# Moving one small tile so that the tiles behind it start at multiples of 128 bytes

## The chip, the cores and the metric

The kernel runs on one core of a Trainium2 chip. The metric is the time of one execution on the device in microseconds (us). The kernel before takes 977.99 us, the median of three runs (977.63 to 978.67). In the profile PE is TensorE's matmuls, PEld its weight loads (LDWEIGHTS), DVE VectorE, ACT ScalarE, POOL GpSimd, SP SyncE, whose queue issues most DMAs.

## The reference

An attention over 32 inducing vectors, a second one back to the tokens, and two MLPs without bias, each with a hidden width of 2048, for 12480 tokens of width 128:

```python
def mab(q, kv):
    s = scale * (q @ kv.transpose(0, 2, 1))
    s = s - s.max(-1, keepdims=True)
    a = np.exp(s)
    a /= a.sum(-1, keepdims=True) + 1e-09
    return a @ kv
h = mab(I, x)                    # I: 32 x 128
x = mab(x, h)                    # 12480 x 128
h = x @ w_in;   x = (h * np.cos(h)) @ w_out                      # MLP 1
h = x @ w_in2;  x = (h * (1.0 / (1.0 + np.exp(-h)))) @ w_out2    # MLP 2
```

The weights come in as float64 and are narrowed on the core.

## The kernel before

The tokens are cut into 98 tiles of 128 (the last has 64). A prologue (up to about 49 us) loads x, transposes it into the tiles xF, held (as x1) and xT, runs the first attention, and multiplies its result h, kept as hT4, with the first MLP's input weights. The four tiles hw0 to hw3 hold that product, so the second attention's output needn't be formed: the main loop multiplies hw with stk, the second attention's weights for a block of tokens.

The main loop works on 26 blocks of tokens. 22 of them are 512 columns wide; of the last four, two are 320 and two are 288 wide. Each block has 8 units, a unit being 256 of the 2048 hidden channels, in two halves. One step of the loop holds, in this order on TensorE:

- `mlp1_in` (line 739): 2 matmuls of unit s, stationary hw, moving stk
- `mlp2_in` (line 878): 6 matmuls of unit s - 11, stationary wi2, moving yhi and ylo
- `mlp2_out` (line 825, in `down`): 6 matmuls of unit s - 13, stationary wo2, moving hi2 and lo2
- `mlp1_out` (line 825, in `down`): 6 matmuls of an earlier unit (s - 1), stationary wo1, moving hi1 and lo1

Between them ACT and DVE form h cos h and its split into hi and lo (lines 782, 788, 794, 815), and ACT and POOL form the Silu and its split (893, 901, 902). A product is of two float32r numbers, each split into a high and a low part, and takes three matmuls for each half: first weights with hi, second weights with hi, first weights with lo. So wo1 is two tiles, wo1_0 and wo1_1, and so are wo2 and wi2. The first 12 units of MLP 1 and the first 8 of MLP 2 use plain float32 weights instead (wf1, and held as wf2; line 835). Six times in the loop the softmax of a further chunk of tokens is worked in ("take" multiplies hT4 with columns of held or xT); around these steps the order of the groups differs, since `mlp2_in` is then held back behind `mlp2_out` or behind `mlp1_out`.

The order is written out by hand (`manual_schedule`). The tiles that live through the whole program come from one pool, `persist`, which lays them out in the order in which they are asked for and rounds each up to a multiple of 32 bytes in a partition. `flag` is one number that the end of the prologue writes (a bound on the size of the cosine's argument); all engines read it once, at line 1037, to choose between the two forms of the main loop.

Of the kernel before, what the change touches and what calls it, by code (L numbers as in the profile page):

```python
# [11 lines left out]
I32 = mybir.dt.int32  # L12
# [9 lines left out]
def tile_induced_attention_then_two_mlps(  # L22
# [58 lines left out]
    persist = ctx.enter_context(tc.tile_pool(name="persist", bufs=1))  # L81

    half_pi = persist.tile([P, 1], F32, name="half_pi")
    quarter = persist.tile([P, 1], F32, name="quarter")
    s_w = persist.tile([P, 1], F32, name="s_w")
    hT4 = persist.tile([C, G, M], F32, name="hT4")

    held = persist.tile([P, G * W], F32, name="held")
# [3 lines left out]
    wf1 = persist.tile([P, NF, C], F32, name="wf1")  # L92
    hw = [persist.tile([P, FF // 4], F32R, name=f"hw{i}") for i in range(4)]
    wo1 = [persist.tile([P, NF, C], F32R, name=f"wo1_{i}") for i in range(2)]
    flag = persist.tile([1, 1], I32, name="flag")
    stk = persist.tile([P, 2, W], F32R, name="stk")

    sft = {
# [980 lines left out]
```

## Time and profile before

| | |
|---|---|
| median of three runs | 977.99 us (977.63 to 978.67) |
| span of the profiled execution | 977.7 us |
| PE (matmuls) busy | 960.4 us, 98% |
| PEld (weight loads) busy | 772.6 us, 79% |
| DVE busy | 787.5 us, 81% |
| ACT busy | 702.6 us, 72% |
| POOL busy | 508.7 us, 52% |
| chain that ended last | PE 95%, DVE 3%, ACT 1%, POOL 1% |
| granted TensorE clock, mean | 0.998 |

A matmul's record lasts longer than its share of the engine, since the next one starts before it ends. So the busy time says that PE is never without work, and the start times of the timeline say at what rate it does it. The timeline merges neighbours of one group; it gives the start of the first and their count. Both `mlp2_out` and `mlp1_out` are line 825 there: in a step the first group of 4 + 2 is wo2, the second is wo1.

### The profile page before, as it was taken

What the parts mean: (1) busy time and instruction counts of PE and PEld (TensorE: products, weight loads), DVE (VectorE), ACT (ScalarE), POOL (GpSimd) and SP (SyncE); (2) the same over time, 40 slices, a digit from 0 to 9 for tenths busy, and PEclk for the clock granted to TensorE, in tenths of its full rate; (3) what the DMA queues carried; (4) which work ended last, traced back from release to release, by engine and by line L of the source; (5) the groups of instructions that cost most, each with busy time, mean ns of one, the idle gap of its engine ahead of it and who ended that gap; (6) DMA issues with size and microseconds to landing.
All of it is one profiled execution on the core that took longest, in us unless ns stands there. A gap on an engine that the chain in (4) does not pass through costs nothing.

```text
span 977.7 us, 12404 instructions
## 1 busy us (share of the span) xinstructions
PE 960.4 (98%) x4663; PEld 772.6 (79%) x4663; DVE 787.5 (81%) x818; ACT 702.6 (72%) x764; POOL 508.7 (52%) x265
## 2 busy tenths in 40 slices
PE   8898999999999999999999999999999999999997
PEld 6544677888887888887888887888887888889997
DVE  4888887988878888888888888888888888867881
ACT  5777677777667777767777776877766877777775
POOL 1234454664554655555655555555555555565555
PEclk9999999999999999999999999999999999999999
DMA  9331010010010010010100100100100100000000
GB/s 352 107 117 49 18 22 5 7 33 11 12 22 6 17 22 5 18 22 1 23 19 4 22 17 5 22 12 11 22 11 12 22 11 8 18 17 12 14 8 17
DMA packets 65230, 28.22 MB, mean 29 GB/s; under 512 B 54312, under 2 KB 59784, under 8 KB 65160
## 3 DMA queue, kind: packets, MB, share of 16 engines
q1 hardware_dynamic: 64504, 27.24, 10.7%
q8 instruction: 39, 0.64, 0.3%
q14 instruction: 31, 0.25, 0.1%
q10 hardware_dynamic: 656, 0.09, 0.1%
HBM read 14.79 MB, written 6.39 MB: 22 GB/s over the span
## 4 chain that ended last, share of the span: by engine, by line
PE 95%; DVE 3%; ACT 1%; POOL 1%; issue 0%; ACTq 0%; POOLq 0%
PE acc L825 52%; PE h L878 27%; PE h L739 9%; PE acc L835 3%; PE pt L371 1%; PE hp L519 1%; PE s L201 1%; PE s L404 1%; PE spin L327 0%; DVE sign L147 0%; ACT c L782 0%; POOL held L155 0%; ACT s L893 0%; DVE sign L144 0%; DVE hi L794 0%
## 5 line engine op out<-in xcount | busy, mean ns | idle before, releaser
L902 POOL TENSOR_TENSOR lo<-s,hi 128x1024 fp32r<-128x1024 f32 (+2 forms) x197 | 448.4, 2276 | 379.8 <-ACT hi L901 353.8
L825 PE MATMUL acc<-hi,wo 128*128 128x512 f32 (+2 forms) x1584 | 409.7, 380 | 0.0
L825 PEld LDWEIGHTS acc<-hi,wo 128*128 128x128 f32 x1584 | 288.2, 188 | 58.8 <-issue 3.4
L788 DVE TENSOR_TENSOR h<-h,c 128x1024 f32<-128x1024 f32 (+2 forms) x196 | 227.5, 1161 | 130.4 <-ACT c L782 130.0
L782 ACT ACTIVATE c<-h,half_pi 128x1024 f32<-128x1024 f32 (+2 forms) x208 | 221.5, 1065 | 150.2 <-PE h L739 150.2
L893 ACT ACTIVATE s<-h 128x1024 f32<-128x1024 f32 (+2 forms) x208 | 202.5, 973 | 73.6 <-PE h L878 68.3
L878 PE MATMUL h<-yhi,wi 128*128 128x512 f32 (+2 forms) x832 | 246.8, 378 | 3.9 <-ACT s L893 3.9
L825 PE MATMUL acc<-lo,wo 128*128 128x512 f32 (+2 forms) x792 | 235.4, 378 | 0.1
L794 DVE CAST hi<-h 128x1024 fp32r<-128x1024 f32 (+2 forms) x196 | 226.2, 1154 | 6.8
L815 DVE TENSOR_TENSOR lo<-h,hi 128x1024 fp32r<-128x1024 f32 (+2 forms) x196 | 225.1, 1149 | 5.7
L901 ACT CAST hi<-s 128x1024 fp32r<-128x1024 f32 (+2 forms) x197 | 196.8, 999 | 6.3
L878 PEld LDWEIGHTS h<-yhi,wi 128*128 128x128 f32 x832 | 152.2, 188 | 33.7 <-ACT s L893 4.8
L825 PEld LDWEIGHTS acc<-lo,wo 128*128 128x128 f32 x792 | 145.7, 188 | 29.9 <-POOL lo L907 0.4
L878 PE MATMUL h<-ylo,wi 128*128 128x512 f32 (+2 forms) x416 | 157.1, 378 | 0.0
L739 PE MATMUL h<-stk,hw 128*128 128x512 f32 (+2 forms) x416 | 127.0, 386 | 2.0 <-DVE c L788 1.3
L739 PEld LDWEIGHTS h<-stk,hw 128*128 128x128 f32 x416 | 76.0, 188 | 26.8 <-issue 7.1
L878 PEld LDWEIGHTS h<-ylo,wi 128*128 128x128 f32 x416 | 78.2, 188 | 14.5
L859 ACT CAST yhi<-acc 128x512 fp32r<-128x512 f32 (+2 forms) x26 | 14.6, 560 | 15.7 <-PE acc L825 13.9
L925 DVE STREAM_TRANSPOSE o<-acc 128x512 f32<-128x512 f32 (+2 forms) x26 | 17.5, 674 | 6.8 <-PE acc L825 6.8
L835 PE MATMUL acc<-c,wf 128*128 128x512 f32 x48 | 22.5, 591 | 0.0
L860 DVE TENSOR_TENSOR ylo<-acc,yhi 128x512 fp32r<-128x512 f32 (+2 forms) x26 | 16.9, 650 | 5.1 <-ACT yhi L859 5.1
L155 POOL TENSOR_TENSOR win<-sign,tail 128x512 int32<-128x512 int32 x4 | 5.1, 1281 | 27.3 <-DVE sign L147 20.8
(143 smaller groups left out, 344.3 us busy)
## 6 DMA issues: line engine op xcount, KB each, us to landing
out_dram<-o SPq DMA_DIRECT2D x80, 64.0 KB, 1.9
x_sb<-in_x_dram SPq DMA_DIRECT2D x8, 512.0 KB, 9.6
raw<-in_moe_w_in_dram SPq DMA_DIRECT2D x8, 512.0 KB, 5.6
raw<-in_moe_w_out_dram SPq DMA_DIRECT2D x8, 512.0 KB, 3.8
stk<-ahi SPq DMA_DIRECT2D x40, 64.0 KB, 2.0
stk<-at SPq DMA_DIRECT2D x40, 64.0 KB, 2.0
x_sb<-in_x_dram SPq DMA_DIRECT2D x3, 256.0 KB, 3.6
x_sb<-in_x_dram SPq DMA_DIRECT2D x2, 320.0 KB
```

The source lines that it names most:

```text
L739: nc.tensor.matmul(ps[:, a, 0:n], lhsT=hw[f // 4][:, f % 4 * P : (f % 4 + 1) * P], rhs=stacks[b][:, 0:n], start=True, stop=True,)
L782: nc.scalar.activation(cs, h, AF.Sin, bias=half_pi, scale=1.0)
L788: nc.vector.tensor_tensor(cs if whole else h, h, cs, ALU.mult)
L794: nc.vector.tensor_copy(hi[:, :, 0:n], h)
L815: nc.vector.tensor_tensor(lo[:, :, 0:n], h, hi[:, :, 0:n].bitcast(F32), ALU.subtract)
L825: nc.tensor.matmul(acc[:, 0:n], lhsT=wt[:, 2 * j + a, :], rhs=gt[:, a, 0:n], start=(j == 0 and p == 0 and a == 0), stop=(j == NJ - 1 and p ...
L835: nc.tensor.matmul(acc[:, 0:n], lhsT=w[:, 2 * j + a, :], rhs=c[:, a, 0:n], start=(j == 0 and a == 0), stop=(j == NJ - 1 and a == 1),)
L878: nc.tensor.matmul(ps[:, a, 0:n], lhsT=wt[:, fs], rhs=yt[:, 0:n], start=(p == 0), stop=(p == 2),)
L893: nc.scalar.activation(sv, hid2.pop(u)[:, :, 0:n], AF.Silu)
L901: nc.scalar.copy(hv, sv)
L902: nc.gpsimd.tensor_tensor(lv, sv, hv.bitcast(F32), ALU.subtract)
L925: nc.vector.transpose(o.rearrange("p t d -> p (t d)")[:, 0:n], acc2.pop(b)[:, 0:n])
```

## The change

The line that asks for `flag` moves from behind `wo1` to ahead of `hT4`:

```diff
     s_w = persist.tile([P, 1], F32, name="s_w")
+    flag = persist.tile([1, 1], I32, name="flag")
     hT4 = persist.tile([C, G, M], F32, name="hT4")
 ...
     wo1 = [persist.tile([P, NF, C], F32R, name=f"wo1_{i}") for i in range(2)]
-    flag = persist.tile([1, 1], I32, name="flag")
     stk = persist.tile([P, 2, W], F32R, name="stk")
```

The instructions, their order and their waits are the same in both built programs. The start addresses within a partition, in bytes, are:

| tile | before | past a multiple of 128 | after | past a multiple of 128 |
|---|---|---|---|---|
| half_pi, quarter, s_w | 16512, 16544, 16576 | 0, 32, 64 | the same | |
| flag | 95968 | 96 | 16608 | 96 |
| hT4 | 16608 | 96 | 16640 | 0 |
| held | 17120 | 96 | 17152 | 0 |
| xT | 25312 | 96 | 25344 | 0 |
| wf1 | 63200 | 96 | 63232 | 0 |
| hw0 to hw3 | 71392, and on by 2048 | 96 | 71424, and on by 2048 | 0 |
| wo1_0, wo1_1 | 79584, 87776 | 96 | 79616, 87808 | 0 |
| stk | 96000 | 0 | the same | |
| hi1, lo1, hi2, lo2, yhi, ylo | 132992 to 192384 | 0 | the same | |
| wi2_0, wi2_1 | 196480, 204672 | 0 | the same | |
| wo2_0, wo2_1 | 212864, 221056 | 0 | the same | |

One LDWEIGHTS of hw, wo1, wi2 or wo2 reads 128 columns, which are 512 bytes of a partition, at a multiple of 512 bytes from its tile's start.

## Rows read from the trace of the kernel before

**Rows 1.** The page: busy us by engine; granted clock in 40 slices; chain that ended last.

```profile
PE 960.4 (98%) x4663; PEld 772.6 (79%) x4663; DVE 787.5 (81%) x818; ACT 702.6 (72%) x764; POOL 508.7 (52%) x265
...
PEclk9999999999999999999999999999999999999999
...
PE 95%; DVE 3%; ACT 1%; POOL 1%; issue 0%; ACTq 0%; POOLq 0%
```

**Rows 2.** Busy time in 640 to 740 us: length, engines (instructions), clock, DMA, GB/s.

```profile
640.00:740.00 100.00, 100.00 (x437) 81.76 (x436) 83.31 (x72) 71.21 (x69) 53.90 (x23) 1.00 0.08 17
```

**Rows 3.** Timeline of PE, one wide step: start us, length us, line, tiles, count.

```profile
797.16 0.62 PE L739 MATMUL h<-stk,hw 128*128 128x512 f32 x2
797.62 0.63 PE L878 MATMUL h<-yhi,wi 128*128 128x512 f32 x2
...
798.31 0.62 PE L878 MATMUL h<-yhi,wi 128*128 128x512 f32 x2
...
798.99 1.07 PE L825 MATMUL acc<-hi,wo 128*128 128x512 f32 x4
...
800.35 1.10 PE L825 MATMUL acc<-hi,wo 128*128 128x512 f32 x4
...
801.75 0.62 PE L739 MATMUL h<-stk,hw 128*128 128x512 f32 x2
```

**Rows 4.** Timeline of PE, the start of hw's group in two steps eleven apart.

```profile
792.57 0.39 PE L739 MATMUL h<-stk,hw 128*128 128x512 f32 x1
...
843.09 0.39 PE L739 MATMUL h<-stk,hw 128*128 128x512 f32 x1
```

**Rows 5.** Groups by line and shape: count, busy us, mean ns, idle us before.

```profile
L825 PEld LDWEIGHTS acc<-hi,wo 128*128 128x128 f32 x1584 | 288.2, 188 | 58.8 <-issue 3.4 <-DVE h L788 1.0 <-DVE hi L794 0.5
...
L878 PEld LDWEIGHTS h<-yhi,wi 128*128 128x128 f32 x832 | 152.2, 188 | 33.7 <-ACT s L893 4.8 <-ACT wi L181 0.2 <-issue 0.2
...
L739 PEld LDWEIGHTS h<-stk,hw 128*128 128x128 f32 x416 | 76.0, 188 | 26.8 <-issue 7.1 <-DVE c L788 3.4 <-ACT stk L682 0.9
```

**Rows 6.** Timeline of PE, a step with narrow MLP 1 and wide MLP 2.

```profile
882.47 0.75 PE L825 MATMUL acc<-hi,wo 128*128 128x320 f32 x4
...
883.35 0.46 PE L739 MATMUL h<-stk,hw 128*128 128x320 f32 x2
883.64 0.61 PE L878 MATMUL h<-yhi,wi 128*128 128x512 f32 x2
...
885.00 1.07 PE L825 MATMUL acc<-hi,wo 128*128 128x512 f32 x4
```

**Rows 7.** Timeline of PE, a step at a softmax chunk, with wo2 behind hw.

```profile
171.92 0.63 PE L739 MATMUL h<-stk,hw 128*128 128x512 f32 x2
172.39 1.09 PE L825 MATMUL acc<-hi,wo 128*128 128x512 f32 x4
...
173.77 0.62 PE L878 MATMUL h<-yhi,wi 128*128 128x512 f32 x2
...
175.13 1.10 PE L825 MATMUL acc<-hi,wo 128*128 128x512 f32 x4
```

**Rows 8.** Timeline of PE behind a hold-up: wo2's group, wi2's, then wo1's.

```profile
149.26 1.09 PE L825 MATMUL acc<-hi,wo 128*128 128x512 f32 x4
...
150.65 0.62 PE L878 MATMUL h<-yhi,wi 128*128 128x512 f32 x2
...
152.03 0.86 PE L825 MATMUL acc<-hi,wo 128*128 128x512 f32 x3
```

**Rows 9.** Groups by line and shape, other engines on moved and unmoved tiles.

```profile
L155 POOL TENSOR_TENSOR tail<-sign,tail 128x512 int32<-128x512 int32 x4 | 5.1, 1287 | 6.4 <-DVE sign L147 6.4
...
L155 POOL TENSOR_TENSOR wf<-sign,tail 128x512 int32<-128x512 int32 x4 | 5.1, 1280 | 22.1 <-DVE sign L147 19.8 <-ACT tail L141 2.3
...
L181 ACT CAST wi<-tail 128x512 fp32r<-128x512 f32 x4 | 2.5, 616 | 0.6 <-POOL tail L155 0.6
L181 ACT CAST wo<-wf 128x512 fp32r<-128x512 f32 x4 | 2.5, 614 | 0.0
```

## The prediction

> **What bounds the kernel now.** I read the page first: its busy shares, the granted clock and the chain that ended last [rows 1]. TensorE's matmuls are busy for 960.4 of 977.7 us, the clock is at its upper level (2.4 GHz) in all 40 slices, and 95% of the chain is PE. The window view of a steady stretch [rows 2] says the same more sharply: in 100 us PE is busy for 100.00, DVE for 83.31, ACT for 71.21, POOL for 53.90, and the DMA engines have a share of 0.08. So in the main loop only the distance from one matmul's start to the next one's counts. I call it the spacing. A busy PE says nothing of it, since matmuls overlap (one is recorded with some 390 ns and the next starts 230 ns after it), so the third view is the timeline of PE alone, whose start times give the spacing.
>
> One step of the loop is 20 matmuls of 512 columns in four groups [rows 3]. From start to start they take: hw (L739, 2 matmuls) 797.16 to 797.62 = 0.46 us, wi2 (L878, 6) 797.62 to 798.99 = 1.37, wo2 (L825, the first 6) 798.99 to 800.35 = 1.36, wo1 (L825, the last 6) 800.35 to 801.75 = 1.40. Per matmul that is 230, 228, 227 and 233 ns. wo1 and wo2 run the same line with the same shapes and both read moving tiles at multiples of 128 bytes, and yet wo1 costs 0.04 us a step more. Within wi2 the first three matmuls take 0.69 us (797.62 to 798.31) and the last three 0.68. Over eleven steps [rows 4] a step is (843.09 - 792.57) / 11 = 4.593 us.
>
> **What the change does.** The built program has the same instructions in the same order with the same waits; only addresses change. Ten tiles, from hT4 to the second wo1, move 32 bytes up, from 96 past a multiple of 128 to a multiple; the flag takes the gap of 32 bytes that this leaves ahead of hT4. Of what the main loop touches in every step, two sets of tiles move: hw and wo1, both stationary operands of TensorE. Everything else in the loop (stk, the hi and lo tiles, yhi and ylo, wi2, wo2, raw) stays where it is, at multiples of 128. So the trace of before holds the comparison already: weights at 96 (hw, wo1) against weights at 0 (wi2, wo2), in one loop at one clock.
>
> *The load itself.* LDWEIGHTS is recorded with 188 ns for L739, L825 and L878 alike [rows 5]. No difference is to be seen there, and it lies beside the matmul before it. If the address costs anything it is in the spacing.
>
> *The spacing by weights.* wo2 at 0: 1.36 / 6 = 226.7 ns. wo1 at 96: 1.40 / 6 = 233.3. For wi2 at 0 the question is why it is not at 226.7 too. Where the blocks are 320 columns wide for hw and wo1 and still 512 for wi2 and wo2 [rows 6], wi2 takes 883.64 to 885.00 = 1.36, so 226.7 as well. And in a step whose order is changed by a softmax step [rows 7], where wo2 and not wi2 stands behind hw, it is wo2 that is slow (172.39 to 173.77 = 1.38) and wi2 that is at the floor (173.77 to 175.13 = 1.36). So the extra goes with hw and wo1 and with the few matmuls right behind them, whichever tile those read, and not with the place in the step or with what DVE, ACT and POOL do at that moment. I take 226.7 ns as the spacing that a train of weights at multiples of 128 settles at.
>
> *The sum.* At 226.7 a step is 20 x 0.2267 = 4.533 us; it is 4.593 now; the gain is 0.060 us. Steps in which hw, wi2, wo2 and wo1 all run with 512 columns: 22 wide blocks of 8 units less the 12 plain-fp32 units at the front, 164. 164 x 0.060 = 9.8 us. The front steps that run hw and wi2 only gain 0.46 + 1.37 - 8 x 0.2267 = 0.016 each, about 0.2 us for 12. The narrow blocks gain nothing: wo1 and hw together take 882.47 to 883.64 = 1.17 us for 8 matmuls of 320 columns, 146 ns, and 0.29 of it is hw at 145. Against it stands a transient: after each hold-up of PE at a softmax step a train starts slow (1.39 + 1.38 us for 12 matmuls [rows 8], 0.05 above the floor); I allow ten such trains (two for each of five softmax steps in the wide part), 0.5 us, which stay as they are. 9.8 + 0.2 - 0.5 = **9.5 us**.
>
> *The rest.* Other instructions that touch moved tiles run in the prologue and the first blocks. ACT's cast to wo1 from wf1 (both at 96) takes 614 ns, to wi2 from tail (both at 0) 616; POOL's join to wf1 1280, to tail 1287 [rows 9]. That is bounded by -7 and +2 ns an instruction over a few dozen, under 0.3 us either way; I take 0, nearest to ACT's pair. No DMA reads or writes a moved tile. The flag is read once per engine at the branch; its address is still a multiple of 4, and I take 0.
>
> *What is late next.* A step shorter by 1.3% puts DVE at 83.31 / 0.987 = 84.4% and ACT at 72% [rows 2]; neither becomes the bound, so the gain is not caught by a wait.
>
> The profiled span is 977.7 us, 0.3 below the median of 977.99, so a gain out of the trace can be taken off the median: 977.99 - 9.5 = **968.5 us**.
>
> **The rivals.**
>
> *B, the address is not what costs.* hw and wo1 differ from wi2 and wo2 in more than 96 bytes: they lie low in the partition (71 to 96 KB against 196 to 229 KB) and are read against other moving tiles (stk, hi1, lo1). If one of these makes the 233 ns, it stays, and the time is 977.99 + 0. For it: no tile of the trace lies low and at a multiple of 128, so rows can't part the two; and the load's 188 ns [rows 5] don't see the address. Against it: hw and wo1 are six tiles at six places between 71 and 88 KB, read against different moving tiles, and both sets are above 226.7. The Trainium skill (SBUF — State Buffer, Specifications (TRN2)) gives SBUF 16-byte lines and a penalty for each step to a new one. By that rule a row of 512 bytes that starts at 96 covers as many lines as one that starts at 0, nothing changes and the time is 978.0, which is this rival. The trace speaks against it only so far as wo1 and wo2, both on 16-byte boundaries, differ by 7 ns.
>
> *C, the slow train stays: slower.* There is a second spacing for weights at 0. Behind a hold-up wo2 and wi2 run at 1.39 + 1.38 us for 12 matmuls = 231 ns [rows 8], and in the steps of rows 3 the train is back at 226.7 within a few matmuls. If the return is owed to the mixture of groups in a step, and with all weights alike nothing pulls the train back, every matmul is at 231: 20 x 0.231 = 4.62 us a step, 0.027 more than 4.593, x 164 = +4.4 us, **982.4**. It decides the other way from a spacing above 4.593 / 20 = 229.7 ns. Against it: in all wide steps the train of wi2 and wo2 does come back to 226.7 within three to twelve matmuls, and nothing in the rows shows it leaving again without a hold-up.
>
> *D, half of it.* Only the loads' own extra goes (wo1 to 1.36, 0.04 a step) and the transient behind hw stays, because it comes from hw's short group or the change of moving tile: 164 x 0.04 = 6.6 less the 0.5 as above, some 6 us, 972.
>
> **How the numbers follow.** Forecast A (968.5; itself 966 to 971, since start times are rounded to 10 ns and an error of 0.015 us in the step's 4.533 is 2.5 us over 164 steps): 0.70. D 0.07, B 0.14, C 0.09. The range goes from the low end of A over D and B, 966.0 to 979.0, and leaves out C and a little of A's tails. What a measurement of this kernel can tell from no change is about 0.2%, 2 us. Faster 0.70 + 0.07 = 0.77, same 0.14, slower 0.09.
>
> **What would show it.** Right: in the timeline of PE a wide step takes 4.53 to 4.54 us, wo1's group 1.36 as wo2's does, wi2 1.36 also behind hw; LDWEIGHTS still 188 ns; DVE's share in the steady window up by a point. Wrong in favour of B: the four groups unchanged at 0.46, 1.37, 1.36 and 1.40. C: all groups near 1.39. D: wo1 at 1.36 and wi2 still at 1.37 or more. The reasoning falls as a whole if the step shortens and the time doesn't, which would mean a wait that these rows don't show.

## The result and the profile after

The changed kernel takes 984.22 us (median of 4 runs, 983.55 to 984.89), the kernel before 978.00 (977.63 to 978.67). The ratio is 1.0061, with an interval of 1.0049 to 1.0073. The change makes the kernel slower by 6.2 us. The forecast was 968.5, in a range from 966.0 to 979.0.

The page of the profiled execution, span 982.0 us. The rows answer to [rows 1]: busy time of the engines, granted clock, the chain by engine.

```profile
PE 964.1 (98%) x4663; PEld 772.1 (79%) x4663; DVE 787.1 (80%) x818; ACT 703.6 (72%) x764; POOL 508.9 (52%) x265
PEclk9999999999999999999999999999999999999999
PE 95%; DVE 3%; ACT 1%; POOL 1%; issue 0%; ACTq 0%; POOLq 0%
```

The window of [rows 2] again, 640 to 740 us, and the groups of weight loads of [rows 5]:

```profile
640.00:740.00 100.00, 100.00 (x433) 81.05 (x432) 82.62 (x71) 70.25 (x68) 53.62 (x23) 1.00 0.08 17
```

```profile
L825 PEld LDWEIGHTS acc<-hi,wo 128*128 128x128 f32 x1584 | 289.2, 188 | 62.5 <-issue 3.5 <-DVE h L788 1.0
...
L739 PEld LDWEIGHTS h<-stk,hw 128*128 128x128 f32 x416 | 75.9, 188 | 25.9 <-issue 7.1 <-DVE c L788 3.3 <-ACT stk L682 0.9
```

Nothing new ends the chain. PE is still busy for all 100 us of the window, at the same clock, and the loads are still recorded with 188 ns. Only the rate differs: 433 matmuls fit where 437 did. DVE and ACT are a little less busy (82.62 and 70.25 us against 83.31 and 71.21), as fewer steps fall into the same 100 us.

Where the time went is seen in PE's timeline, one wide step as in [rows 3], then the start of hw's group in two steps that are sixteen apart as in [rows 4], then the narrow step of [rows 6] with the groups ahead of it (wo1 and hw, 320 columns each). Columns are start, length, line, tiles, count.

```profile
673.58 0.63 PE L739 MATMUL h<-stk,hw 128*128 128x512 f32 x2
674.05 0.64 PE L878 MATMUL h<-yhi,wi 128*128 128x512 f32 x2
...
675.45 1.08 PE L825 MATMUL acc<-hi,wo 128*128 128x512 f32 x4
...
676.83 1.10 PE L825 MATMUL acc<-hi,wo 128*128 128x512 f32 x4
...
678.22 0.63 PE L739 MATMUL h<-stk,hw 128*128 128x512 f32 x2
...
753.30 0.63 PE L739 MATMUL h<-stk,hw 128*128 128x512 f32 x2
...
827.52 0.63 PE L739 MATMUL h<-stk,hw 128*128 128x512 f32 x2
...
881.97 0.76 PE L825 MATMUL acc<-hi,wo 128*128 128x320 f32 x4
...
882.86 0.46 PE L739 MATMUL h<-stk,hw 128*128 128x320 f32 x2
883.15 0.63 PE L878 MATMUL h<-yhi,wi 128*128 128x512 f32 x2
...
884.54 1.09 PE L825 MATMUL acc<-hi,wo 128*128 128x512 f32 x4
```

From start to start the groups take 0.47 us (hw), 1.40 (wi2), 1.38 (wo2) and 1.39 (wo1). Before they took 0.46, 1.37, 1.36 and 1.40 [rows 3]. A step is (827.52 - 753.30) / 16 = 4.639 us, against 4.593 [rows 4]. So wo1, which was to come down to 1.36, came down by 0.01 only, and the groups whose tiles didn't move got slower: wi2 by 0.03, wo2 by 0.02. In the narrow step wo1 and hw together take 883.15 - 881.97 = 1.18 us, as before (1.17), and yet wi2 behind them takes 884.54 - 883.15 = 1.39 us, where it took 1.36 [rows 6].

The same over the whole trace, from the starts of all float32r matmuls of 512 columns (distances above 250 ns, which are hold-ups, left out): hw 227.9 to 233.3 ns, wi2 229.1 to 232.7, wo2 227.3 to 229.7, wo1 233.7 to 232.4. All together (3357 of them after the change) go from 229.79 to 231.77 ns, which is 1.98 x 3357 = 6.6 us, the measured 6.2 within the scatter of the runs.

Taken by place in the step, over the 134 wide steps without a hold-up in each trace: before, hw's own two matmuls take 0.454 us together, 227.1 ns each, and the slow ones are wo1's six and the first three of wi2 (231.7, 232.5 and 230.8 ns); the fourth of wi2 is at 226.7. After, hw is at 233.6, and the floor isn't reached before the fourth matmul of wo2, the tenth behind hw.

### The profile page after: what moved, and what is told of

It reads as the page before. It is cut to its first block, busy times and chain, and to the rows that moved or that the text cites. A ratio compares the mean times of both kernels' runs of the same rounds, so it can differ in the third digit from the quotient of the medians.

```text
span 982.0 us, 12404 instructions
## 1 busy us (share of the span) xinstructions
PE 964.1 (98%) x4663; PEld 772.1 (79%) x4663; DVE 787.1 (80%) x818; ACT 703.6 (72%) x764; POOL 508.9 (52%) x265
## 4 chain that ended last, share of the span: by engine, by line
PE 95%; DVE 3%; ACT 1%; POOL 1%; issue 0%; ACTq 0%; POOLq 0%
PE acc L825 52%; PE h L878 27%; PE h L739 9%; PE acc L835 2%; PE pt L371 1%; PE hp L519 1%; PE s L201 1%; PE s L404 1%; PE spin L327 0%; DVE sign L147 0%; ACT c L782 0%; POOL held L155 0%; ACT s L893 0%; DVE sign L144 0%; DVE hi L794 0%
## 5 line engine op out<-in xcount | busy, mean ns | idle before, releaser
L739 PE MATMUL h<-stk,hw 128*128 128x512 f32 (+2 forms) x416 | 129.0, 392 | 2.0 <-DVE c L788 1.3
```

Of the source, the lines that this page charges most:

```text
L739: nc.tensor.matmul(ps[:, a, 0:n], lhsT=hw[f // 4][:, f % 4 * P : (f % 4 + 1) * P], rhs=stacks[b][:, 0:n], start=True, stop=True,)
```

## The experiments

The prediction had two sets of tiles move to multiples of 128 and compared "at 96" with "at 0". The comparison left out that each matmul has a second operand, the moving tile, with an address of its own. The tiles' places in the built programs, as remainders by 256:

| | hw | wo1 | stk | wi2, wo2 | yhi, ylo, hi1, lo1, hi2, lo2 |
|---|---|---|---|---|---|
| before | 224 | 224 | 0 | 128 | 128 |
| after | 0 | 0 | 0 | 128 | 128 |

In both programs the groups that were at the floor of 226.7 ns before, wi2 behind its first three matmuls and wo2, have weights and moving tile at the same remainder. wo1 lies 96 above its moving tiles before and 128 from them after. hw lies 32 below stk before, and level with it after.

**Weights alone, at every 32 bytes.** A kernel with nothing but trains of 32 float32r matmuls of 512 columns, weights at w and moving tile at a fixed place (remainder 128):

```
for w in (0, 32, 64, ...):
    for n in range(32):
        matmul(acc, lhsT=weights at w, rhs=moving, 512 columns)
```

> Leaves the whole computation out: zeros go to the output, and TensorE runs 108 trains of 32 float32r matmuls (128x128 weights, 512 columns) with no other engine at work. First 32 trains: the weights' start goes through all multiples of 32 bytes mod 1024, the moving tile stays at 896. Next 32: the moving tile goes through them and the weights stay at 896. Next 32: the first again, backwards. Last 12: steps of 4 to 32 bytes from 896. Theory T1 (what counts is how the weights' and the moving tile's addresses stand to one another): trains at 226.7 ns a matmul only at equal residues (some power of two up to 1024), 230 to 240 elsewhere, whichever of the two moves. Theory T2 (the weights' own start mod 128, as predicted, with a slow train that may hold): the weights at multiples of 128 give 226.7 or 231, other starts 231 to 238, and moving the moving tile changes nothing. Theory T3 (addresses don't count, the tiles' neighbours in the loop do): all trains alike.

Timeline of PE in this kernel, a train a row; tab has its weights at remainder 32, tac at 64, and so on to tah at 224, tai at 0 again. The start of the next row less a row's own start is the time of 32 matmuls.

```profile
15.87 7.63 PE L53 MATMUL tab<-moving,weights 128*128 128x512 f32 x32
23.34 7.50 PE L53 MATMUL tac<-moving,weights 128*128 128x512 f32 x32
30.68 7.63 PE L53 MATMUL tad<-moving,weights 128*128 128x512 f32 x32
38.15 7.42 PE L53 MATMUL tae<-moving,weights 128*128 128x512 f32 x32
45.41 7.62 PE L53 MATMUL taf<-moving,weights 128*128 128x512 f32 x32
...
60.34 7.64 PE L53 MATMUL tah<-moving,weights 128*128 128x512 f32 x32
67.82 7.59 PE L53 MATMUL tai<-moving,weights 128*128 128x512 f32 x32
```

tad, at 96, takes 38.15 - 30.68 = 7.47 us, tae, at 128, 45.41 - 38.15 = 7.26, tah 67.82 - 60.34 = 7.48. By the last 20 matmuls of each train (the first few still carry what came before) the spacing is 232.4 ns at 0, 233.1 to 233.5 at 32, 228.9 at 64, 233.35 at 96, 226.65 at 128, 233.3 at 160 and 192, 234.15 at 224, and so on again every 256 bytes. Being at a multiple of 128 is thus not what gives 226.7: of the two kinds of such multiples one does, the other has 232.4. Where the moving tile moves instead of the weights, the same differences (weights less moving tile) give the same values within 0.4 ns, but for 128: there the trains have 231.95 to 233.35, and the same two addresses 232.4 in the trains with the weights' starts rising and 231.95 in those with them falling. Starts between the multiples of 32 bytes are not better: with the weights 4, 8, 16 and 24 bytes above the moving tile it is 232.65, 230.65, 233.3 and 230.0, and with the moving tile 4 bytes above the weights 236.65, the slowest of all.

**The parts of the change.** wo1 alone moves (hw stays at 224):

```
-    wo1 = [persist.tile([P, NF, C], F32R, name=f"wo1_{i}") for i in range(2)]
     flag = persist.tile([1, 1], I32, name="flag")
+    wo1 = [persist.tile([P, NF, C], F32R, name=f"wo1_{i}") for i in range(2)]
     stk = persist.tile([P, 2, W], F32R, name="stk")
```

> The flag's tile stands between hw and wo1: wo1 is at a multiple of 128 as in the changed kernel, hw and all ahead of it at 96 as before. T1: wo1 at 768 mod 1024 against hi1 and lo1 at 896 is what slowed the changed kernel; about as slow as it, 982 to 985 us, hw's group 0.46 us. T2: wo1 alone at a multiple of 128; if the slow train is owed to hw, 968 to 972 us, else 984. T3: 978.

It takes 978.65 us, ratio 1.0008 [0.9999, 1.0016]. Timeline of PE, a step from hw to hw, with wo1's group last:

```profile
674.36 0.62 PE L739 MATMUL h<-stk,hw 128*128 128x512 f32 x2
...
677.55 1.10 PE L825 MATMUL acc<-hi,wo 128*128 128x512 f32 x4
...
678.95 0.62 PE L739 MATMUL h<-stk,hw 128*128 128x512 f32 x2
```

The step is 4.59, and wo1 takes 678.95 - 677.55 = 1.40 us with its weights at a multiple of 128 and of 256. This is the direct answer to the forecast's main term: wo1's 0.04 us a step is not to be had there. T1's 982 to 985 didn't come either: wo1 alone is not what slows the changed kernel.

hw alone moves (wo1 stays at 224, though 8192 bytes lower):

```
-    hw = [persist.tile([P, FF // 4], F32R, name=f"hw{i}") for i in range(4)]
     wo1 = [persist.tile([P, NF, C], F32R, name=f"wo1_{i}") for i in range(2)]
     flag = persist.tile([1, 1], I32, name="flag")
+    hw = [persist.tile([P, FF // 4], F32R, name=f"hw{i}") for i in range(4)]
     stk = persist.tile([P, 2, W], F32R, name="stk")
```

> wo1, then the flag's tile, then hw: hw is at a multiple of 128 (768 mod 1024) as in the changed kernel, wo1 at 96 (736 mod 1024) as before, though 8192 bytes lower. T1: hw at 768 and stk at 768 are equal, so hw's group gets no slower than 0.46 us and the time is 976 to 979 us. T2: hw's short group at 0, wo1 as before: 976 to 979 us, and if hw's group holds the train slow behind it, 981 to 985. T3: 978.

It takes 981.72 us, ratio 1.0040 [1.0027, 1.0053]. Timeline of PE, one step: hw, wi2, wo2, wo1, hw.

```profile
676.94 0.62 PE L739 MATMUL h<-stk,hw 128*128 128x512 f32 x2
677.39 0.63 PE L878 MATMUL h<-yhi,wi 128*128 128x512 f32 x2
...
678.78 1.08 PE L825 MATMUL acc<-hi,wo 128*128 128x512 f32 x4
...
680.16 1.10 PE L825 MATMUL acc<-hi,wo 128*128 128x512 f32 x4
...
681.56 0.62 PE L739 MATMUL h<-stk,hw 128*128 128x512 f32 x2
```

681.56 - 676.94 = 4.62 us. hw's own group is hardly slower than before (0.459 us against 0.454 over 134 wide steps), but wi2 behind it takes 1.39 and wo2 1.38 (1.37 over the 134). Two matmuls of a step set how the twelve behind them run. With hw at 0 alone this is 3.9 us of the whole, with both moved 6.2; wo1 alone is 0.8 with an interval that reaches to 0. So the parts don't add up to the whole, and T1, which took each matmul by its own pair of addresses and expected 976 to 979 here, missed too. Nor does it fit hw before: 32 below its moving tile, which is 233.3 ns in a train, it has 227.1 in the step.

Is the slow wo1 ahead of hw needed for this? A narrow step of the same run, wo1 and hw with 320 columns, wi2 and wo2 with 512:

```profile
875.92 0.75 PE L825 MATMUL acc<-hi,wo 128*128 128x320 f32 x4
...
876.80 0.45 PE L739 MATMUL h<-stk,hw 128*128 128x320 f32 x2
877.10 0.63 PE L878 MATMUL h<-yhi,wi 128*128 128x512 f32 x2
...
878.49 1.09 PE L825 MATMUL acc<-hi,wo 128*128 128x512 f32 x4
```

wo1 and hw take 877.10 - 875.92 = 1.18 us for 8 matmuls, no slow train, and wi2 behind them 878.49 - 877.10 = 1.39, where it took 1.36 before [rows 6]. So wi2 can be slow behind hw without a slow wo1 ahead. In the wide step, where wo1 is slow in all of these kernels, no run parts the two.

**Addresses alone, without the kernel.** One kernel with a map of 8 weights places by 8 moving places, and behind it the loop's step as 20 matmuls, with the six placings of hw, stk and wo1 that matter, 12 steps each. No DVE, ACT or POOL work is in it:

```
for name, (hw, stk, wo) in CASES.items():      # remainders by 256
    hw group: 2 matmuls, weights at hw, moving at stk
    wi2 group: 6, both at 128
    wo2 group: 6, both at 128
    wo1 group: 6, weights at wo, moving at 128
```

> Leaves the whole computation out: zeros go to the output. First 64 trains of 32 matmuls: the moving tile's start (slow index, letters a to h for 0, 32 .. 224 mod 256) against the weights' start (fast index). Then the 20 matmuls of the loop's step, twelve times over, with no other engine at work, for six layouts of hw, stk and wo1 mod 256 (wi2, wo2 and all other moving tiles at 128): before (224, 0, 224), after (0, 0, 0), wozero (224, 0, 0), hwzero (0, 0, 224), best (128, 128, 128), stkzero (128, 0, 128). Theory T1 (the distance of the weights' start from the moving start mod 256 sets the spacing): 226.7 ns on the diagonal, 229 where the weights start 64 bytes below, 232 to 234 elsewhere; steps of 4.59 us for before, 4.64 for after, 4.59 wozero, 4.62 hwzero, 4.53 for best. Theory T3 (other engines or PSUM take part): the layouts' steps alike, or far from those in the kernel.

In the map the eight pairs with the same remainder have 226.65 to 226.7 ns (227.25 in the first train, whose first matmuls take 427 ns), the pairs with weights 64 below the moving tile 228.85 to 228.9, those 128 apart 232.35 to 232.5 and once 233.3, those with weights 96 above 234.1 to 234.15, all others 233.1 to 233.45 (last 20 matmuls of each train). So within such a train the spacing follows the weights' start less the moving tile's start, modulo 256, to within 0.4 ns but for the pairs 128 apart. Timeline of PE, the start of hw's group in two steps running, in four of the six placings:

```profile
510.54 0.62 PE L47 MATMUL before_hw<-moving,weights 128*128 128x512 f32 x2
515.13 0.62 PE L47 MATMUL before_hw<-moving,weights 128*128 128x512 f32 x2
...
561.28 0.63 PE L47 MATMUL after_hw<-moving,weights 128*128 128x512 f32 x2
565.92 0.63 PE L47 MATMUL after_hw<-moving,weights 128*128 128x512 f32 x2
...
676.62 0.62 PE L47 MATMUL hwzero_hw<-moving,weights 128*128 128x512 f32 x2
681.24 0.62 PE L47 MATMUL hwzero_hw<-moving,weights 128*128 128x512 f32 x2
...
713.41 0.62 PE L47 MATMUL best_hw<-moving,weights 128*128 128x512 f32 x2
717.94 0.62 PE L47 MATMUL best_hw<-moving,weights 128*128 128x512 f32 x2
```

Steps of 4.59, 4.64, 4.62 and 4.53 us, as in the kernels. Over several steps the six placings have 4.593 (before), 4.640 (after), 4.593 (wo1 at 0), 4.620 (hw at 0), 4.553 (hw and wo1 at 128, stk at 0) and 4.533 (all three at 128); the means of the 134 undisturbed wide steps in the six kernels' traces are the same to 0.001. So in a wide step the addresses of TensorE's two operands, in the order of the step, make the whole difference; no other engine has a part in it.

**All at one remainder.** Four small tiles of 32 bytes go behind stk, so that hw, wo1 and stk all lie at 128, as everything else in the loop does:

```
-    half_pi = persist.tile([P, 1], F32, name="half_pi")
-    quarter = persist.tile([P, 1], F32, name="quarter")
-    s_w = persist.tile([P, 1], F32, name="s_w")
     hT4 = persist.tile([C, G, M], F32, name="hT4")
...
-    flag = persist.tile([1, 1], I32, name="flag")
     stk = persist.tile([P, 2, W], F32R, name="stk")
+    half_pi = persist.tile([P, 1], F32, name="half_pi")
+    quarter = persist.tile([P, 1], F32, name="quarter")
+    s_w = persist.tile([P, 1], F32, name="s_w")
+    flag = persist.tile([1, 1], I32, name="flag")
```

> All four small tiles stand behind stk, so that hw, wo1 and stk start at 128 mod 256 like wi2, wo2 and the other moving tiles. T1: every matmul of the loop at 226.7 ns, a step of 4.53 us, 0.06 x 164 = 9.8 us less than before: 967 to 970 us. T2 (only the weights' start mod 128 counts): like the changed kernel, 982 to 985. T3: 978.

It takes 969.25 us (967.95 to 970.71), ratio 0.9910 [0.9897, 0.9924] to the kernel before, and is faster than both kernels. One wide step of the timeline of PE (hw, wi2, wo2, wo1, hw), then wi2 and the start of wo2 in a narrow step:

```profile
673.09 0.61 PE L739 MATMUL h<-stk,hw 128*128 128x512 f32 x2
673.55 0.62 PE L878 MATMUL h<-yhi,wi 128*128 128x512 f32 x2
...
674.91 1.07 PE L825 MATMUL acc<-hi,wo 128*128 128x512 f32 x4
...
676.27 1.07 PE L825 MATMUL acc<-hi,wo 128*128 128x512 f32 x4
...
677.63 0.62 PE L739 MATMUL h<-stk,hw 128*128 128x512 f32 x2
...
873.37 0.63 PE L878 MATMUL h<-yhi,wi 128*128 128x512 f32 x2
...
874.76 1.07 PE L825 MATMUL acc<-hi,wo 128*128 128x512 f32 x4
```

Every group of the wide step is at the floor: 0.46, 1.36, 1.36, 1.36, and wo1 lies in the same low part of the partition as before and after. In the narrow step wi2 takes 874.76 - 873.37 = 1.39 us behind hw's 320 columns, where it took 1.36 before, although weights and moving tile agree in every matmul: five slow matmuls stand behind the narrow group here, none did before.

**Two sizes in between.** The small tiles (half_pi, quarter, s_w) between wo1 and stk leave stk at 0 and put hw and wo1 at 128:

```
-    half_pi = persist.tile([P, 1], F32, name="half_pi")
-    quarter = persist.tile([P, 1], F32, name="quarter")
-    s_w = persist.tile([P, 1], F32, name="s_w")
     hT4 = persist.tile([C, G, M], F32, name="hT4")
...
     wo1 = [persist.tile([P, NF, C], F32R, name=f"wo1_{i}") for i in range(2)]
+    half_pi = persist.tile([P, 1], F32, name="half_pi")
+    quarter = persist.tile([P, 1], F32, name="quarter")
+    s_w = persist.tile([P, 1], F32, name="s_w")
     flag = persist.tile([1, 1], I32, name="flag")
```

> The four small tiles stand between wo1 and stk: hw and wo1 at 128 mod 256, stk at 0 as before and after. T1: wo1's group at 1.36 us, hw's pair and the load of wi2 behind it run against stk at a distance of 128, and the slow start behind them reaches into wi2: a step of 4.55 to 4.57, 971 to 975 us. T2: 982 to 985.

972.36 us, ratio 0.9946 [0.9932, 0.9959]. And hw and wo1 at 64, the one distance of the map that costs little, with stk at 128:

```
+    flag = persist.tile([1, 1], I32, name="flag")
+    m2_ = persist.tile([P, KT, 1], F32, name="m2")
     hT4 = persist.tile([C, G, M], F32, name="hT4")
...
-    flag = persist.tile([1, 1], I32, name="flag")
+    sm_ = persist.tile([P, KT, 1], F32, name="sm")
     stk = persist.tile([P, 2, W], F32R, name="stk")
...
-        "m2": persist.tile([P, KT, 1], F32, name="m2"),
-        "sm": persist.tile([P, KT, 1], F32, name="sm"),
+        "m2": m2_,
+        "sm": sm_,
```

> Small tiles are dealt out so that hw and wo1 start at 64 mod 256 and stk at 128: hw and wo1 are 64 bytes below what they are multiplied with, neither at a multiple of 128. T1: 228.9 ns for these 8 matmuls, 226.7 for the other 12 and a short transient, a step of 4.55 to 4.57: 970 to 974 us. T2: weights off a multiple of 128 like those of before, 978 or more.

974.03 us, ratio 0.9965 [0.9952, 0.9979], at the upper end of what T1 expected. Timeline of PE, hw's group in two steps running, stk at 0 first, then hw and wo1 at 64:

```profile
673.63 0.62 PE L739 MATMUL h<-stk,hw 128*128 128x512 f32 x2
...
678.18 0.62 PE L739 MATMUL h<-stk,hw 128*128 128x512 f32 x2
```

```profile
671.92 0.62 PE L741 MATMUL h<-stk,hw 128*128 128x512 f32 x2
...
676.50 0.62 PE L741 MATMUL h<-stk,hw 128*128 128x512 f32 x2
```

Steps of 4.55 and 4.58 us (means 4.553 and 4.573) lie between 4.53 and 4.59, in the order that the map gives. They lie above 4.533 by 0.020 and 0.040 us, though, about twice what the map's pairs add up to (2 x 5.7 ns = 0.011, 8 x 2.2 ns = 0.018); the rest is in the matmuls behind the pairs that disagree. With the mean spacing of all float32r matmuls of 512 columns in each trace, against 229.79 ns before, the five edits and the change stand so:

| kernel | mean spacing, ns | difference x 3357, us | measured by the ratio, us |
|---|---|---|---|
| the change | 231.77 | +6.6 | +6.0 |
| hw at 0 alone | 230.94 | +3.9 | +3.9 |
| wo1 at 0 alone | 229.78 | 0.0 | +0.8 |
| hw, wo1 at 64, stk at 128 | 228.79 | -3.4 | -3.4 |
| hw, wo1 at 128, stk at 0 | 227.98 | -6.1 | -5.3 |
| hw, wo1, stk at 128 | 227.02 | -9.3 | -8.8 |

**Which pair of operands counts.** Two ideas were left for what happens inside a mixed step: each matmul's own weights and moving tile, or the next matmul's weights, which are loaded while this one runs, against this one's moving tile. A kernel of trains that alternate between two places tells them apart, and trains with other widths and types stand behind:

```
train("same",     [(0, 0), (128, 128)])   # (weights, moving) of each matmul in turn
train("crossed",  [(128, 0), (0, 128)])
train("sameb",    [(0, 0), (96, 96)])
train("crossedb", [(96, 0), (0, 96)])
```

> Leaves the whole computation out: zeros go to the output. Trains of 32 matmuls, no other engine at work. Same: weights and moving tile of one matmul agree mod 256, both alternate between 0 and 128 (sameb: 0 and 96), so the next weights are 128 (96) off the tile that streams. Crossed: weights and moving tile of one matmul differ by 128 (96), and the next weights agree with the tile that streams. Theory P (the load of the next weights runs beside the stream of the current moving tile, and these two must agree): same 232 to 234 ns, crossed 226.7. Theory Q (the two operands of one matmul must agree): same 226.7, crossed 232 to 234. Then distance 0, 96 and 128 with 512, 448, 384, 320 and 288 columns: if the cost is a fixed number of ns a matmul, 6 to 7 ns more at 96 and 128 whatever the columns; by the narrow blocks of the kernel, nothing at 320 and 288. Then plain float32 (by the kernel's 428 ns rows at 96 off: no difference) and bfloat16 (open).

Timeline of PE, a train of 32 a row:

```profile
15.85 7.48 PE L53 MATMUL same<-moving,weights 128*128 128x512 f32 x32
23.17 7.52 PE L53 MATMUL crossed<-moving,weights 128*128 128x512 f32 x32
30.53 7.67 PE L53 MATMUL sameb<-moving,weights 128*128 128x512 f32 x32
38.04 7.52 PE L53 MATMUL crossedb<-moving,weights 128*128 128x512 f32 x32
```

Neither idea holds. By the last 20 matmuls "same" has 228.3 ns and "crossed" 230.0, where one of them should have had 226.7 and the other 232.4; with places 96 apart they have 234.0 and 230.0. What a matmul pays in a mixed sequence is thus not given by one pair of operands. This stays open.

## Why the prediction was wrong

What held, by its own steps. Matmul spacing alone bounds the main loop: PE is busy for 100.00 of 100 us after as before, and the mean spacing accounts for every kernel in the table within 0.8 us. The load's 188 ns doesn't see the address. The sum from step to kernel held too: a step of 4.533 us was to give some 9.5 us, and where the wide step does become 4.533, with all three at 128, the kernel gains 8.8. No wait of another engine catches that gain: beyond the spacing, the distances above 250 ns hold 14.4 us there (52 of them) against 14.0 before (45). A term that the forecast had at nothing, the narrow blocks, takes a little back: in ten steps wi2 loses 0.025 us each.

The step that failed is the one that reads the weights' address out of [rows 3, 6, 7]: "I take 226.7 ns as the spacing that a train of weights at multiples of 128 settles at". The rows show that wo1 differs from wi2 and wo2. But the two sets differ in more than the weights' distance to a multiple of 128. The sentence that set them side by side, that both wo groups "read moving tiles at multiples of 128 bytes", stopped at 128, and at 256 the rows part: wi2 and wo2 lie level with what they are multiplied with, wo1 doesn't. Put to 0, wo1 goes from 96 above its moving tile to 128 from it, 234.15 and 232.4 ns in the trains. So the term of 0.04 us a step was 0.01.

The other half of the miss is hw. The forecast's 230 ns for it is 0.46 / 2, a start time rounded to 10 ns; over 134 steps it is 227.1, so hw itself had next to nothing to gain, and of the argument against rival B that "both sets are above 226.7" only wo1 is left. Level with stk, hw should by its own pair have stayed near the floor. With it at 0, however, the matmuls behind it stay slow for longer, up to the third of wo2 where it had been the third of wi2: over the whole trace wi2 goes from 229.1 to 232.7 ns, wo2 from 227.3 to 229.7, and the forecast had both at 226.7. In the narrow steps this needs no slow wo1 ahead; in the wide ones it isn't shown whether it does. That the placing does this is shown, by hw moved alone and by the train of 20 matmuls without the rest of the kernel. By which step inside TensorE's pipeline is not.

The rivals. C, the slow train stays, gave 982.4 us and groups near 1.39, and something near it came: 984.2, with 1.40, 1.38 and 1.39. It had a chance of 0.09. Its price came near because the prediction took it from a slow train of the kernel before, 231 ns [rows 8], and the mean after the change is 231.77; that it fits is luck, since its reason doesn't hold. C held that the mixture of places pulls the train back and that likeness keeps it slow. With all three at one place and level, the train of the wide steps is at its fastest. B, that something other than this address makes the 233 ns, was right in that the moving tile matters; in the time it was wrong, since B has nothing change. That hw and wo1 lie low in the partition has no effect: they lie there at 227.2 and 226.9 ns too, with all at 128. D asked for wo1 at 1.36, which didn't come. It comes with hw and wo1 at 128 and stk at 0: wo1 1.36 and wi2 1.375 over 134 steps, and 972.36 us, D's 972. In the wide steps the slow start behind hw goes as soon as stk is at 128 as well, so it was owed to stk's place, and not to hw's short group or the change of moving tile as such.

The evidence against C was weak: "nothing in the rows shows it leaving again without a hold-up". In [rows 3] the train leaves 226.7 at wo1, without a hold-up, and the return behind it takes several matmuls. The return was read as a property of wi2 and wo2, when it also depended on what hw left behind.

## What to carry to other kernels

Where a loop is bound by float32r matmuls of 512 columns, look at the start addresses of both operands of each matmul modulo 256, not at one operand modulo some power of two, and try all tiles of the loop at one remainder: here that was 0.9% for the place of four small tiles, and the fastest of the layouts that were run. Agreement group by group wasn't enough: hw level at 0 between groups level at 128 made those slower. Before a difference between two groups is put down to one address, list every address in which they differ. The place of a group of two matmuls can cost more in the groups behind it than in itself, so move one group at a time, and don't expect the parts to add up.

## What the runs showed of the hardware

The spacing of float32r matmuls of 512 columns at the upper clock is 226.65 ns in a train where the starts of weights and moving tile agree modulo 256, and up to 234.35 at other multiples of 32 bytes, 3.4% more; 4 bytes off it was 236.65. What an address costs depends on width and type. At 448 columns a distance of 96 is the fastest, 200.0 ns against 202.65 at 0 and 204.0 at 128; at 320 columns all three have 146.7, as the narrow groups in [rows 6] already did with weights at 96. Plain float32 has 429.2 ns per recorded matmul at distances 0, 96 and 128, and bfloat16 215.8 at each of six distances.

The Trainium skill (TensorE: Matmul & The Clock Gate, Back-to-back issue gap) gives N / 2.4 + 2.5 ns as the gap between single matmuls at the upper clock, which is 215.8 for 512 columns. The bfloat16 trains agree with it; the float32r trains, at 226.65 and more, don't. The rule of 16-byte lines that the prediction set beside rival B (the Trainium skill, SBUF — State Buffer, Specifications (TRN2)) would have all starts that are multiples of 16 alike; the trains in steps of 32 bytes, between 226.65 and 234.35, speak against its being all that counts here.

A train keeps something of what ran before it: behind a group with other distances an agreeing group needs several matmuls to come to 226.7, behind narrow groups sometimes too (five with all at 128, none before), and trains that alternate between two agreeing places have 228.3 (0 and 128) and 234.0 (0 and 96) to the end of their 32 matmuls. No run here shows what holds this.
